# Pacing the attention stage's transfers by bytes instead of by planned time, with new instruction orders

## The chip, the cores and the metric

The kernel runs on one core of one Trainium2 chip. The metric is device time in microseconds (us) of one execution. A core has five instruction streams that matter here: PE (TensorE, matrix products), DVE (VectorE), ACT (ScalarE), POOL (GpSimd) and SP (SyncE, which here only issues transfers). All bulk transfers leave from SP's queue and are carried out by 16 DMA engines.

## What is computed

Decay attention for 8 batches, 8 heads, 576 positions and a head size of 64, and on its output a two-part mixer: one product pair along the positions, one along the channels.

```python
scores = scale * np.matmul(q, k.transpose(0, 1, 3, 2))
cum = np.cumsum(np.log(np.clip(f, 0.0001, 1.0)), axis=-1)
decay = cum[:, :, :, None] - cum[:, :, None, :]
scores = np.where(causal, -1000000000.0, scores + decay)
attn = np.exp(scores - np.max(scores, axis=-1, keepdims=True))
attn = attn / (np.sum(attn, axis=-1, keepdims=True) + 1e-09)
x = np.matmul(attn, v)                      # then (B, S, H * D)
...
h = np.maximum(x.transpose(0, 2, 1) @ w_tok1, 0.0) @ w_tok2
u = x + h.transpose(0, 2, 1)
return u + np.maximum(u @ w_ch1, 0.0) @ w_ch2
```

The channel weights come as 64-bit floats, and everything is kept to float32 precision.

## The kernel before

There are two stages. The **attention stage** takes the 64 heads as 32 pairs. For each pair SP loads q and k (`raw`, 576 KB), v (`vr`, two loads of 160 KB) and, for 26 of the pairs, a broadcast decay bias (`cb`, 576 KB). PE makes scores (L745), DVE adds the bias and takes the row minimum of the negated scores (L786), ACT takes the exponential and its row sums (L790), PE transposes (L860), ACT and DVE copy the transposed blocks out of PSUM (L870, L868) and PE multiplies by v (L889). After each second pair the inverse sums go out to memory (`recd<-rs`, L838, 5 KB each) and come back broadcast (`rb<-recd`, L843, 320 KB each), and POOL multiplies with them (L920). After each fourth pair the first mixer runs on PE (L1260, L1243), and its result goes to memory (`ud<-xt`, L1329). Beside all this the 24 weight blocks of the channel mixer are decoded from 64-bit floats: SP loads `d_raw` (L557), ACT, DVE and POOL convert (L570 to L590, L629), and the result is written back as `wd<-sg` (L638). The **channel stage** from about 405 us on streams these blocks back (`wq<-wd`, L960) into seven-product matrix multiplications (L1045 to L1047 and L1126 to L1128).

Each engine's instruction order is fixed in advance: `ORDER` (L27 on) lists, for PE, DVE, ACT, POOL and SP, the numbers of the steps in the order in which they are issued. `Plan.run` (L312) walks these lists with modelled durations. That decides which buffer slot each step gets, and so the waits between engines; the order on an engine itself comes from the table alone.

SP issues strictly in order. A transfer whose buffer is not yet free, or whose data are not yet written, holds back all transfers behind it. On top of this comes **pacing** (L318 to L328): each transfer of the attention stage may only be issued after an earlier transfer of the same queue has landed, called its hold. The loop keeps a sum `ahead` of the planned durations (`lat`, bytes divided by an assumed rate) of the transfers between the hold and the transfer, and picks as hold the latest transfer that still leaves at least `AHEAD` = 4500 ns of planned work between. The assumed rate is 300 bytes per ns for most transfers (L483), 247 for `vr` and 235 for `rb`. L1498 and L1499 turn the hold into a semaphore wait. Transfers of the channel stage have no hold.

Of the kernel before, what the change touches and what calls it, by code (L numbers as in the profile page):

```python
# [24 lines left out]
AHEAD, AHEAD_TO = 4500.0, 8  # L25
# [42 lines left out]
    ),  # L68
    DVE=(
# [187 lines left out]


class Op:
    __slots__ = ("eng", "dur", "head", "tail", "lat", "fn", "bufs", "need", "outs", "ready", "start", "idx", "port", "mode", "hold", "at_sp", "got")  # L260


class Plan:
# [48 lines left out]
    def run(self, slots):  # L312
# [6 lines left out]
        for k, o in enumerate(sent):  # L319
            if k > 1:  # L320
                ahead += sent[k - 1].lat
# [117 lines left out]
def build(nc, env, dims):  # L439
# [9 lines left out]
    p = Plan()  # L449
# [1084 lines left out]
```

## Time and profile before

| | |
|---|---|
| time, median of 3 runs | 933.07 us (929.41 to 933.65) |
| the profiled execution | 933.73 us |
| its span, first to last instruction | 931.9 us |
| PE busy, share of the span | 911.5 us, 98% |
| DVE, ACT, POOL busy | 709.0, 523.0, 234.8 us |
| moved by DMA | 242.49 MB, mean 260 GB/s |
| granted TensorE clock, mean | 0.999 of full speed |

The profiled execution lies 0.66 us above the median, and 1.8 us of it lie around the span. Busy times of different engines overlap, so they don't add up to the span; a busy PE can still contain short stalls inside a run of instructions. Waits of SP ("SPq") are waits of the issuing queue, not of the DMA engines.

### The profile page before, as it was taken

To read this page: it belongs to the slowest core of one execution; us is meant where nothing else is said; L and a number is where in the kernel's file an instruction comes from. 1 tells how busy PE (TensorE), PEld (TensorE's weight loads), DVE (VectorE), ACT (ScalarE), POOL (GpSimd) and SP (SyncE) were. 2 spreads that over 40 slices of the span, in tenths; PEclk is the share of its full clock that TensorE was granted. 3 is DMA by queue.
4 is the path that set the end of the run, shared out by engine and by line. 5 is a ranking of instruction groups with operands and counts; after the bars stand their busy time and mean duration, and the time that the engine had idled before them with its cause. 6 is when DMAs were issued, how large, how long until landed. Compare 5 with 4: busy or idle time off the path is not lost.

```text
span 931.9 us, 26826 instructions
## 1 busy us (share of the span) xinstructions
PE 911.5 (98%) x10270; PEld 794.3 (85%) x10270; DVE 709.0 (76%) x1894; ACT 523.0 (56%) x1340; POOL 234.8 (25%) x320
## 2 busy tenths in 40 slices
PE   7999899999999999999999999999999999999998
PEld 5678788888788888988888888888889999999997
DVE  7988878888788778664898369953898359954786
ACT  6979888999888989721463135512353125421242
POOL 4577567676675662100000000000000000000000
PEclk9999999999999999999999999999999999999999
DMA  8989989899998988469799888898879878887774
GB/s 247 250 277 287 308 210 321 290 297 264 301 301 251 288 265 252 134 205 329 237 308 286 269 234 236 261 302 258 261 248 287 275 227 250 248 270 232 241 249 153
DMA packets 145023, 242.49 MB, mean 260 GB/s; under 512 B 19136, under 2 KB 76736, under 8 KB 144896
## 3 DMA queue, kind: packets, MB, share of 16 engines
q1 hardware_dynamic: 144800, 240.64, 84.0%
q8 instruction: 81, 1.33, 0.6%
q14 instruction: 46, 0.38, 0.1%
q10 hardware_dynamic: 96, 0.15, 0.0%
HBM read 199.52 MB, written 41.21 MB: 258 GB/s over the span
## 4 chain that ended last, share of the span: by engine, by line
PE 89%; DVE 6%; DMA 2%; ACT 2%; issue 2%; SPq 0%; DVEq 0%; ACTq 0%
PE bank L1243 11%; PE bank L1045 9%; PE bank L1126 9%; PE bank L1127 9%; PE bank L1128 9%; PE bank L1046 9%; PE bank L1047 9%; PE bank L745 7%; PE bank L889 7%; PE bank L860 5%; DVE pr L786 3%; PE bank L1260 1%; ACT pr L790 1%; DVE pf L868 1%; DMA d_raw<-in_w_tok 1%
## 5 line engine op out<-in xcount | busy, mean ns | idle before, releaser
L487 ACT ACTIVATE st<-H 128x464 fp32r<-128x464 f32 (+1 forms) x210 | 120.7, 587 | 117.4 <-PE bank L1127 78.1
L790 ACT ACTIVATE pr<-pr,nmin 128x192 f32<-128x192 f32 (+4 forms) x320 | 176.5, 558 | 15.2 <-DVE nmin L786 14.9
L1126 PE MATMUL bank<-st,wq 128*128 128x464 f32 (+1 forms) x420 | 156.0, 371 | 0.0
L1127 PE MATMUL bank<-st,wq 128*128 128x464 f32 (+1 forms) x420 | 155.9, 371 | 0.0
L1128 PE MATMUL bank<-st,wq 128*128 128x464 f32 (+1 forms) x420 | 155.7, 371 | 0.0
L786 DVE CUSTOM_DVE_ANT_0 pr<-bank,cb 128x448 f32<-128x448 f32 (+3 forms) x260 | 108.6, 458 | 11.3 <-PE bank L751 6.7
L745 PE MATMUL bank<-raw 64*64 64x448 f32 (+6 forms) x1408 | 111.4, 397 | 5.4 <-issue 1.8
L496 DVE TENSOR_TENSOR st<-H,st 128x464 fp32r<-128x464 f32 (+1 forms) x150 | 92.3, 631 | 13.4 <-ACT st L487 13.3
L981 DVE TENSOR_TENSOR tmp<-bank,tmp 128x464 f32<-128x464 f32 (+1 forms) x80 | 50.3, 633 | 61.6 <-PE bank L1047 46.6
L889 PE MATMUL bank<-pf,vr 64*64 64x128 f32 (+3 forms) x2048 | 96.5, 315 | 0.0
L870 ACT ACTIVATE pf<-bank 128x512 f32<-128x512 f32 x152 | 84.0, 595 | 11.8 <-PE bank L860 6.3
L1128 PEld LDWEIGHTS bank<-st,wq 128*128 128x128 f32 x420 | 78.8, 188 | 9.2
L1126 PEld LDWEIGHTS bank<-st,wq 128*128 128x128 f32 x420 | 78.9, 188 | 9.0
L1127 PEld LDWEIGHTS bank<-st,wq 128*128 128x128 f32 x420 | 78.8, 188 | 8.8
L889 PEld LDWEIGHTS bank<-pf,vr 64*64 64x64 f32 x2048 | 75.2, 133 | 7.7 <-ACT pf L870 1.5
L745 PEld LDWEIGHTS bank<-raw 64*64 64x64 f32 x1408 | 54.5, 133 | 31.7 <-issue 9.8
L1071 ACT ACTIVATE H<-bank 128x464 f32<-128x464 f32 (+1 forms) x30 | 16.5, 555 | 115.2 <-PE bank L1047 109.3
L860 PE MATMUL bank<-ident,pr 64*128 64x64 f32 x1536 | 63.6, 224 | 4.3 <-issue 1.4
L860 PEld LDWEIGHTS bank<-ident,pr 64*128 64x128 f32 x1536 | 58.9, 139 | 8.1 <-DVE nmin L786 2.2
L920 POOL TENSOR_TENSOR xt<-xt,rb 128x64 f32<-128x64 f32 (+1 forms) x64 | 52.4, 837 | 48.0 <-DMA rb<-recd 26.0
L790 ACT ACTIVATION_READ_ACCUMULATOR pr<-pr,nmin 128x1 f32 (+1 forms) x320 | 62.5, 195 | 0.0
L1243 PE MATMUL bank<-t2h,ring 64*128 64x288 f32 x512 | 60.7, 304 | 1.8 <-issue 1.5
(166 smaller groups left out, 2072.8 us busy)
## 6 DMA issues: line engine op xcount, KB each, us to landing
wq<-wd SPq DMA_DIRECT2D x420, 256.0 KB
raw<-in_qk SPq DMA_DIRECT2D x32, 576.0 KB
cb<-decd SPq DMA_DIRECT2D x26, 576.0 KB
d_raw<-in_w_ch SPq DMA_DIRECT2D x48, 256.0 KB
wd<-sg SPq DMA_DIRECT2D x24, 512.0 KB
vr<-in_v SPq DMA_DIRECT2D x64, 160.0 KB
rb<-recd SPq DMA_DIRECT2D x32, 320.0 KB
wd<-sg SPq DMA_DIRECT2D x24, 384.0 KB
```

The lines of the kernel that those rows point to most:

```text
L487: nc.scalar.activation(out, in_, func, scale=scale)
L496: nc.vector.tensor_tensor(out, in_, asf(hi), op=ALU.subtract)
L745: nc.tensor.matmul(at(buf)[HALF[h], of : of + n], q[:, i0 : i0 + D], k[:, j0 : j0 + n], start=t not in (0, 1), stop=not nd, skip_group_che ...
L786: nc.vector.tensor_tensor_reduce(o, x, y, -1.0 / D**0.5, c0[:m, NS + z : NS + z + 1] if t == 5 else 3e38, op0=ALU.add, op1=ALU.min, accum_ ...
L790: nc.scalar.activation(x, x, AF.Exp, bias=E["nmin"][sm][:m, t : t + 1], scale=-1.0, accum_out=E["rec"][rm][:m, c : c + 1])
L860: nc.tensor.transpose(at(ps[s])[:, k * D : (k + 1) * D], at(pr)[r, x, :, :].rearrange("p a b -> p (a b)"), E["ident"][r, r])
L870: p.op("ACT", d_act(512), lambda src_=src_, o=o: nc.scalar.activation(o(), src_(), AF.Copy), rd=[ps[s]], wr=[(pt, s)], bufs=[ps[s], pt])
L889: nc.tensor.matmul(at(av[z])[o, 256 - w : 256], at(vr)[r, vblk(j), :], at(pt)[r, c : c + w], start=j == 4, stop=gi == 2, skip_group_check= ...
L1126: nc.tensor.matmul(o, wt[:, 0, :], h_, start=(first and x == 0), stop=False, skip_group_check=True)
L1127: nc.tensor.matmul(o, wt[:, 1, :], h_, start=False, stop=False, skip_group_check=True)
L1128: nc.tensor.matmul(o, wt[:, 0, :], l_, start=False, stop=(x == FX - 1), skip_group_check=True)
L1243: last[s] = nc.tensor.matmul(at(ps[s ^ z])[:, : width[0]], a, m, start=(z == 0 and i == 0), stop=(z == 1 and i == len(todo[s]) - 1), skip_ ...
```

## The change

The pacing no longer adds up planned durations but bytes: each transfer carries its `size`, and the hold is the latest transfer that leaves at least 1,200,000 bytes between. The first transfer of the queue, which the old sum skipped, is now counted. The flag that marks paced steps has a new name and the same condition. All five lists in `ORDER` are replaced.

```diff
-AHEAD, AHEAD_TO = 4500.0, 8
+AHEAD, PACED = 1200000, 8
...
-        "14:12 145 135:2 146 26:2 155 139 28:3 185 156 140 31:11 202 188 42 193 43:6 165 168 171 49 275 267 284 218 174 "
+        "14:12 145 135:2 146 26:2 155 139 28:3 156 185 140 31:12 193 202 43:6 188 49 165 168 171 275 267 284 174:2 211 "
...
-        o.mode, o.hold, o.at_sp = mode, None, self.batch < AHEAD_TO
+        o.mode, o.size, o.hold, o.paced = mode, 0, None, self.batch < PACED
...
-        j, ahead, sent = -1, 0.0, queue["SP"]
+        j, ahead, sent = -1, 0, queue["SP"]
         for k, o in enumerate(sent):
-            if k > 1:
-                ahead += sent[k - 1].lat
-            while j + 1 < k - 1 and ahead - sent[j + 1].lat >= AHEAD:
+            ahead += sent[k - 1].size if k else 0
+            while j + 1 < k - 1 and ahead - sent[j + 1].size >= AHEAD:
                 j += 1
-                ahead -= sent[j].lat
-            if j >= 0 and o.at_sp:
+                ahead -= sent[j].size
+            if j >= 0 and o.paced:
                 o.hold = sent[j]
...
     def dma(fn, nbytes, **k):
-        return p.op("SP", k.pop("dur", 475), fn, lat=nbytes / k.pop("rate", 300), **k)
+        o = p.op("SP", k.pop("dur", 475), fn, lat=nbytes / k.pop("rate", 300), **k)
+        o.size = nbytes
+        return o
```

305 of SP's 910 transfers are paced, in both kernels. Counted with the loop over both orders, the bytes between a hold and its transfer go from a mean of 1.57 MB (1.21 to 1.98) to a mean of 1.44 MB (1.20 to 1.78). Of the step lists, PE has 255 of 940 steps at another place (by 8 places at most), DVE 746 of 1498 (39), ACT 604 of 1020 (28), POOL 246 of 312 (13), SP 292 of 910 (47). From PE's step 2889 on, in the channel stage, PE's list is the same; the other lists agree from about there too. The numbers in buffer names below are slots; lines of the changed kernel below L484 stand two further down (L838 is now L840).

SP, the write of the inverse sums of the tenth and eleventh pair (`recd<-rs0`, at 128.66 us in the trace before), before:

```order
L720 DMA vr0_183<-in_v 64x2x320 x2
L638 DMA wd1_2_130<-sg1_156 128x3x256
L730 DMA cb0_185<-decd_118 128x1152
L838 DMA recd_119<-rs0_96 20x64 x2
L638 DMA wd1_3_131<-sg3_158 128x3x256
L557 DMA d_raw2_152<-in_w_ch1 128x512
L1329 DMA ud1_121<-xt1_145 128x1152
L843 DMA rb0_188<-recd_119 64x1280
L557 DMA d_raw2_152<-in_w_ch1 128x2x256
L843 DMA rb0_188<-recd_119 64x1280
```

SP, the same place, now:

```order
L559 DMA d_raw2_152<-in_w_ch1 128x2x256
L722 DMA vr0_183<-in_v 64x2x320
L840 DMA recd_119<-rs0_96 20x64
L1331 DMA ud1_121<-xt1_145 128x1152
L840 DMA recd_119<-rs0_96 20x64
L732 DMA cb0_185<-decd_118 128x1152
L640 DMA wd1_2_130<-sg1_156 128x4x256
L845 DMA rb0_188<-recd_119 64x1280
L732 DMA cb1_186<-decd_118 128x1152
L845 DMA rb0_188<-recd_119 64x1280
```

The bias load `cb0` has moved from ahead of the two small writes to behind them, the write `ud1` now stands between them, and two loads or writes of weight blocks have moved ahead of them. The bytes ahead of the first small write are 33.8 MB in both.

SP, the reading back of the inverse sums four pairs later (`rb`, at 187.86 us in the trace before), before:

```order
L838 DMA recd_119<-rs2_98 20x64 x2
L638 DMA wd1_5_133<-sg1_156 128x3x256
L557 DMA d_raw0_150<-in_w_ch2 128x2x256
L730 DMA cb0_185<-decd_118 128x1152
L638 DMA wd1_5_133<-sg0_155 128x4x256
L717 DMA raw2_182<-in_qk 128x1152
L557 DMA d_raw2_152<-in_w_ch2 128x2x256
L843 DMA rb0_188<-recd_119 64x1280 x2
```

SP, the same place, now:

```order
L840 DMA recd_119<-rs2_98 20x64
L1331 DMA ud2_122<-xt0_144 128x1152
L840 DMA recd_119<-rs2_98 20x64
L722 DMA vr0_183<-in_v 64x2x320
L640 DMA wd1_4_132<-sg0_155 128x3x256
L640 DMA wd1_5_133<-sg2_157 128x3x256
L559 DMA d_raw0_150<-in_w_ch2 128x2x256
L722 DMA vr0_183<-in_v 64x2x320
L732 DMA cb1_186<-decd_118 128x1152
L845 DMA rb0_188<-recd_119 64x1280
```

The second `d_raw` load no longer stands between the small writes and `rb`, and the next `raw` has moved ahead of the small writes; one `d_raw` load still stands ahead of `rb`.

## Rows read from the trace of the kernel before

**Rows 1.** Busy time and DMA share by stretch; columns: stretch, engines, clock, DMA, GB/s
```profile
0.00:50.00 50.00, 42.28 (x738) 29.40 (x740) 44.30 (x182) 37.60 (x110) 26.36 (x48) 1.00 0.87 257
50.00:100.00 50.00, 48.97 (x1017) 41.79 (x1012) 43.98 (x164) 44.38 (x133) 37.76 (x50) 1.00 0.90 275
100.00:150.00 50.00, 45.37 (x934) 39.39 (x935) 40.98 (x149) 41.16 (x123) 33.32 (x44) 1.00 0.93 274
150.00:200.00 50.00, 49.76 (x1029) 41.41 (x1027) 43.21 (x160) 44.51 (x130) 32.79 (x45) 1.00 0.94 299
200.00:250.00 50.00, 48.93 (x1016) 41.95 (x1016) 41.68 (x148) 45.76 (x137) 33.86 (x44) 1.00 0.94 288
250.00:300.00 50.00, 48.50 (x1030) 40.28 (x1024) 41.94 (x159) 41.91 (x127) 30.57 (x42) 1.00 0.88 270
300.00:350.00 50.00, 49.51 (x1022) 42.51 (x1022) 39.13 (x150) 43.94 (x134) 30.28 (x39) 1.00 0.91 275
350.00:405.00 55.00, 54.92 (x1012) 48.94 (x1014) 37.96 (x119) 39.56 (x113) 9.86 (x12) 1.00 0.68 200
405.00:450.00 45.00, 45.00 (x222) 40.19 (x219) 27.41 (x50) 11.34 (x22) 0.00 (x0) 1.00 0.82 260
450.00:930.00 480.00, 478.25 (x2286) 428.42 (x2284) 348.43 (x622) 172.86 (x318) 0.00 (x0) 1.00 0.83 256
```

**Rows 2.** PE's timeline, its idle times over 1 us between 95 and 135 us
```profile
101.72 0.46 PE L1260 MATMUL bank<-ident,xt 64*128 64x64 f32 x8 [1.78 <-issue]
115.66 0.48 PE L745 MATMUL bank<-raw 64*64 64x320 f32 x4 [1.36 <-issue]
122.66 0.40 PE L1243 MATMUL bank<-t2h,ring 64*128 64x288 f32 x1 [1.48 <-issue]
```

**Rows 3.** Waits of SP's queue, 0 to 405 us: in total, times, longest
```profile
SPq L557 <- DVE d_g L590: 24.7, 12, 4.4
SPq L838 <- DVE rs L831: 24.5, 10, 5.6
...
SPq L638 <- DMA d_raw<-in_w_ch: 8.2, 5, 2.6
SPq L717 <- DMA d_raw<-in_w_ch: 7.8, 5, 2.5
...
SPq L638 <- DMA rb<-recd: 6.6, 5, 2.5
```

**Rows 4.** SP's timeline at four places: start, duration, what
```profile
107.02 0.67 SPq L838 DMA_DIRECT2D recd<-rs  x2
...
112.03 1.13 SPq L843 DMA_DIRECT2D rb<-recd  x2
...
122.55 0.43 SPq L730 DMA_DIRECT2D cb<-decd  x1
128.66 0.68 SPq L838 DMA_DIRECT2D recd<-rs  x2
...
187.27 0.55 SPq L557 DMA_DIRECT2D d_raw<-in_w_ch  x1
...
223.14 0.67 SPq L838 DMA_DIRECT2D recd<-rs  x2
...
226.13 1.26 SPq L843 DMA_DIRECT2D rb<-recd  x2
```

**Rows 5.** The columns of rows 1, by the us, where SP waited
```profile
127.00:128.00 1.00, 1.00 (x19) 0.48 (x19) 1.00 (x4) 0.82 (x3) 1.00 (x2) 1.00 0.15 60
128.00:129.00 1.00, 1.00 (x16) 0.66 (x12) 1.00 (x3) 1.00 (x5) 0.04 (x1) 1.00 0.00 0
129.00:130.00 1.00, 1.00 (x20) 0.81 (x20) 0.52 (x2) 1.00 (x5) 0.00 (x0) 1.00 0.05 10
```

**Rows 6.** DVE's timeline, the first reading of that `cb`
```profile
141.11 0.22 DVE L786 CUSTOM_DVE_ANT_0 pr<-bank,cb 64x64 f32<-64x64 f32 x1
```

**Rows 7.** POOL's timeline, the wait for `rb`
```profile
194.88 3.09 POOL L920 TENSOR_TENSOR xt<-xt,rb 128x512 f32<-128x512 f32 x4 [2.92 <-DMA rb<-recd]
```

**Rows 8.** Waits of PE, 0 to 405 us, the only one for a transfer
```profile
PE bank L745 <- DMA raw<-in_qk: 1.4, 1, 1.4
```

More of the change, by code (lines that the diff above doesn't have):

```diff
@@ L259 @@
 class Op:
-    __slots__ = ("eng", "dur", "head", "tail", "lat", "fn", "bufs", "need", "outs", "ready", "start", "idx", "port", "mode", "hold", "at_sp", "got")
+    __slots__ = ("eng", "dur", "head", "tail", "lat", "fn", "bufs", "need", "outs", "ready", "start", "idx", "port", "mode", "size", "hold", "paced", "got")
 class Plan:
```

397 rows, old and new, of tables (ACT, DVE, PE, POOL) are left out of this document.

## The prediction

> **What bounds the kernel now.** I read the busy times by stretch first [rows 1]. Up to 405 us runs the attention stage, after it the channel stage. In the channel stage PE is busy 45.00 of 45 and 478.25 of 480 us, and its order there is the same but for the first steps, so I look for nothing there. In the attention stage PE's idle time is what the eight rows leave over: 7.72, 1.03, 4.63, 0.24, 1.07, 1.50, 0.49 and 0.08 us, together 16.8 us. The first 7.7 us hold the start, where there is nothing to multiply yet. Of the 4.63 us between 100 and 150 us, 1.78 + 1.36 + 1.48 = 4.62 us are three gaps marked "issue" [rows 2]: PE waited for nothing that the profile shows, no semaphore and no transfer. So without the start and these three, about 4.4 us of plain idle time are left in 405 us. The engines beside PE are full too: between 50 and 350 us DVE is busy 78 to 88% and ACT 82 to 92%, and the DMA engines 88 to 94%, at 270 to 299 GB/s. The stage is four tight engines coupled by small buffers, and PE is the one that ends it.
>
> Then the waits of SP's queue [rows 3], because the change acts there. Two kinds of wait for a compute engine lead: 24.7 us in 12 waits for a weight block's decode, 24.5 us in 10 waits for the inverse sums. Those come from the order. Waits for a transfer, among which are all the holds, come in many small rows; the largest are 8.2, 7.8 and 6.6 us, of five waits each, the longest of a row being 2.5 or 2.6 us. Last, who waits for what SP brings: PE waits for a transfer once in the stage, 1.4 us [rows 8].
>
> **Term 1, pacing by bytes.** Between hold and transfer there are now 1.44 MB on the mean where there were 1.57 MB, and 1.20 MB at least. At 280 GB/s, the middle of the rates in rows 1, the mean difference is 0.13 MB / 280 GB/s = 0.46 us: that much later a transfer is issued where the hold is its last wait. It costs only where the DMA engines run dry meanwhile. What must be covered is the time from a landing to the next transfer's work. The nearest rows: the small write `recd` and the read `rb` that needs it. At 223.14 us the two writes are issued, done at 223.81, and `rb` follows at 226.13: 2.3 us, with other issues between, so an upper bound in a queue with little in it. At 107.02 it is 112.03 - 107.69 = 4.3 us, with a full queue in front, which contains the data of others [rows 4]. With 1.2 MB behind the hold, the engines have 1.2 MB / 280 GB/s = 4.3 us of work, 2.0 us more than the 2.3. So the cover is the transfers already queued, and it is still there at the smallest window. If the cover were gone, the price is 0.46 us for each long wait: the three largest rows hold 15 waits, so 15 x 0.46 = 6.9 us, if each reached PE. That is the upper end. Below zero: a later issue brings no data sooner, but fewer bytes queued could shorten the three issue gaps, if data in the queues is what delays PE there. In proportion (0.13 of 1.57 MB, 8% of 4.62 us) that gains 0.4 us. I take +0.4 us, one exposed delay, near the row of PE's single wait: one in the stage.
>
> Here a rule of the Trainium skill speaks against the change. In "DMA: Bandwidth & Descriptors", section "Anatomy of one DMA — SWDGE (gpsimd) path", a transfer's time is a fixed part of about 2.0 us, mostly completion, and bytes at 436 GB/s. At that rate 1.2 MB would last only 2.75 us, hardly more than the round trip, and the smallest windows would leave the engines dry; by it the sum would take the upper end of term 1 and not its middle. The rate in this trace is 299 GB/s at best over 50 us [rows 1], so the trace does not agree with the rule's rate for this mix of transfers, and its 2.0 us are below the 2.3 us read here.
>
> **Term 2, the orders.** The same instructions run on each engine, so busy time stays, and only waits can change. At the first place SP blocked before `recd` for the inverse sums: `cb` was issued at 122.55, `recd` only at 128.66, a wait of 5.6 us [rows 3, 4], and the DMA engines fell to 0.15, 0.00 and 0.05 of their share from 127 to 130 us, while PE stayed busy for all three us [rows 5]. Now `cb` is behind `recd`, `ud` is between the two small writes, and as many bytes stand ahead of them, so the engines run dry just as before unless the sums come sooner. Behind the waiting `recd` now stand `ud`, the second `recd`, `cb`, `wd` and `rb`. The `cb` that moved back was first read at 141.11 us [rows 6], 18.6 us after its issue; issued at about 130 it still has 11 us, against the 4.3 us that a round trip took in a full queue. I price this move at nothing, hidden by DVE's and PE's earlier work; if that cover is gone, it costs DVE up to the wait's 5.6 us.
>
> At the second place `d_raw` waited for its buffer until 187.27 us, and `rb` stood behind it; POOL waited 2.92 us for `rb` before 194.88 [rows 4, 7]. Now one `d_raw` load less stands between, but another is still ahead. At best POOL gets these 2.92 us back. PE's idle time in that stretch is 0.24 us in all [rows 1], so PE gains 0.24 us at most unless stalls hide inside its busy time. So this too is worth nothing I could measure.
>
> The other moves are too many to price one by one. Their bounds: they cannot gain more plain idle time than there is, 4.4 us, and the largest single loss that rows show is SP's 5.6 us wait coming up once more, with PE behind it. I take 0, since no row names a wait on PE of more than 1.4 us that the order could take away, and because the waits that go at one place come back at another: SP's blocking writes are all still there.
>
> **The sum.** The profiled execution took 933.73 us. Term 1 adds 0.4 and term 2 adds 0: 934.1 us. The profiled execution lies 0.66 us over the median of the runs shown, so for the median I forecast 933.5 us. Its own range goes down by term 2's 4.4 and term 1's 0.8 (from +0.4 to -0.4) to 928.3, and up to 937.7, the point from which a loss would be told from no change and the rivals below begin.
>
> **Rivals.** (A) A new blocked head of SP's queue, slower. In the new order a transfer that PE needs soon gets behind a `recd` or `d_raw` that waits. Price: one 5.6 us wait with the queue dry, all of it reaching PE, 933.1 + 5.6 = 938.7 us. For: 22 such waits stand in the two leading rows, and `ud`, which waits for the mixer's sums, now stands ahead of the second `recd`. Against: PE stayed busy while the engines were dry before, and PE waited for a `raw` once in the stage, 1.4 us [rows 5, 8]. It decides from the point where a `raw` or `cb` lands after its first use would have begun. Chance 0.11.
>
> (B) The window runs dry, slower. The holds of 1.20 MB release too late, and the engines run dry before the next transfer starts. All 15 long waits of term 1 get 0.46 us longer: 933.1 + 6.9 = 940 us. For: SP's waits for transfers grow with load, and the engines are at 88 to 94% already. Against: 2.0 us of cover. It decides where DMA share between 100 and 300 us falls below 0.88 with SP waiting for a transfer. Chance 0.06.
>
> (C) The new orders take out stalls inside PE's busy time, faster. Between 50 and 350 us PE is called busy nearly throughout, but its weight loads are busy 39 to 43 of 50 us [rows 1], so short stalls may hide there. If the orders regain 2% of those 300 us, that is 6 us: 933.1 - 6 = 927 us. For: so many steps moved, on all engines. Against: no one row shows a wait this large on PE. Chance 0.13.
>
> (D) The pacing doesn't do what it says: the holds are so seldom the last wait that the window's size changes nothing, and only the orders act. That gives 933.1 us and falls inside the forecast, so it shares its chance of 0.70.
>
> **How the numbers follow.** What the runs of this kernel can tell from no change is about 0.5%, 4.7 us: 928.4 to 937.7 us. The forecast with D has 0.70, A and B, both over 937.7, have 0.17 together, C has 0.13. So faster 0.13, same 0.70, slower 0.17. For 8 in 10 the range must reach a part of the cases on both sides: 928.5 to 939.5 us leaves out most of C and of B.
>
> **What would show it.** Term 1 is right if SP's waits for transfers keep their sum and DMA share between 100 and 300 us stays at 0.88 to 0.94; wrong if the share falls while those waits grow. Term 2 is right if PE's idle time up to 350 us stays within a few us of 16.7, if SP's wait at `recd` near 128 us is still there, and if POOL's wait near 195 us shrinks without PE noticing. The end of the attention stage near 405 us is the mark: if it moves by more than 4.7 us, the forecast is wrong, and the stretch in which PE's work first runs ahead or behind tells which rival it was.

## The result and the profile after

The changed kernel takes 937.99 us (median of 8 runs, 935.1 to 942.57), the kernel before, run beside it, 933.36 us (median of 8 runs, one of which took 1951.73 us and is left out of the ratio). The ratio is 1.0051, 95% interval 1.0028 to 1.0074: slower by half a per cent. The forecast was 933.5 us with a range of 928.5 to 939.5, so the time lies in the range, but just past the 937.7 us up to which I had called it no change. The profiled execution took 937.82 us, its span is 936.0 us (931.9 before).

Busy time by stretch in the changed kernel: stretch, PE, weight loads, DVE, ACT, POOL (each with its count), granted clock, DMA share, GB/s. Its last three rows are single microseconds.

```profile
0.00:50.00 50.00, 40.85 (x739) 29.06 (x741) 44.31 (x176) 37.27 (x109) 26.61 (x47) 1.00 0.83 254
50.00:100.00 50.00, 48.25 (x955) 41.91 (x955) 43.61 (x159) 42.89 (x130) 35.42 (x47) 0.97 0.86 274
100.00:150.00 50.00, 48.63 (x1009) 41.19 (x1003) 44.16 (x162) 43.68 (x130) 36.42 (x49) 1.00 0.95 279
150.00:200.00 50.00, 48.79 (x998) 39.85 (x1000) 41.62 (x152) 43.76 (x131) 30.47 (x42) 1.00 0.99 296
200.00:250.00 50.00, 49.35 (x1032) 42.76 (x1026) 44.59 (x153) 45.37 (x137) 38.31 (x49) 1.00 0.92 278
250.00:300.00 50.00, 46.64 (x1008) 39.41 (x1003) 40.01 (x150) 39.80 (x120) 28.96 (x40) 1.00 0.98 293
300.00:350.00 50.00, 48.94 (x996) 42.31 (x992) 39.92 (x153) 45.19 (x138) 29.85 (x39) 1.00 0.95 269
350.00:405.00 55.00, 53.94 (x1021) 47.59 (x1022) 37.65 (x124) 39.49 (x115) 10.43 (x12) 1.00 0.63 189
...
127.00:128.00 1.00, 1.00 (x13) 0.29 (x7) 1.00 (x3) 1.00 (x5) 1.00 (x2) 1.00 0.29 95
128.00:129.00 1.00, 1.00 (x24) 0.86 (x26) 1.00 (x4) 1.00 (x4) 1.00 (x1) 1.00 0.47 182
129.00:130.00 1.00, 1.00 (x41) 0.98 (x37) 1.00 (x5) 1.00 (x4) 0.06 (x1) 1.00 1.05 398
```

Against [rows 1], stretch by stretch, PE idles more by 1.43, 0.72, -3.26, 0.97, -0.42, 1.86, 0.57 and 0.98 us: 19.6 us in 405 us where there were 16.8. The clock row adds a part: between 50 and 100 us the granted clock is 0.97 of full speed, because from 53.07 to 56.48 us PE ran at 1.2 and not 2.4 GHz. Those 3.4 us at half rate cost up to 1.7 us. Together that is up to 2.9 + 1.7 = 4.6 us, against 4.1 us more span. The last matrix product of the attention stage ends at 409.3 us and not at 405.6; what is left to the end is 526.7 and 526.3 us. So 3.7 of the 4.1 us are lost in the attention stage.

The waits of SP's queue in the changed kernel, 0 to 405 us: in total, times, longest.

```profile
SPq L559 <- DVE d_g L592: 24.3, 15, 4.0
SPq L840 <- DVE rs L833: 14.8, 7, 4.2
...
SPq L640 <- DMA vr<-in_v: 10.0, 6, 3.0
SPq L640 <- DMA raw<-in_qk: 7.5, 6, 2.7
```

Where [rows 3] had 24.5 us in 10 waits for the inverse sums there are now 14.8 in 7. All waits for transfers together grew from 91.7 us in 90 waits to 118.9 us in 109. On the whole the DMA engines did not run dry for it: their share between 100 and 350 us is 0.92 to 0.99.

SP's timeline of the changed kernel at the two places of the prediction: start, duration, what.

```profile
127.43 0.31 SPq L840 DMA_DIRECT2D recd<-rs  x1
...
128.18 0.36 SPq L840 DMA_DIRECT2D recd<-rs  x1
128.58 0.76 SPq L732 DMA_DIRECT2D cb<-decd  x1
...
184.88 0.47 SPq L845 DMA_DIRECT2D rb<-recd  x1
185.94 0.57 SPq L559 DMA_DIRECT2D d_raw<-in_w_ch  x1
...
188.97 0.60 SPq L845 DMA_DIRECT2D rb<-recd  x1
```

And POOL's wait at the second place:

```profile
196.93 0.60 POOL L922 TENSOR_TENSOR xt<-xt,rb 128x64 f32<-128x64 f32 x2 [4.76 <-DMA d_raw<-in_w_ch]
```

The first place behaves as foreseen: SP still blocks before `recd`, for 2.9 us where it was 5.6 (the profile puts 2.4 us of it down to a `raw` load, but DVE's reciprocal ended only at 126.86 + 0.54 = 127.40 us, just before `recd` went), and the engines still run low (0.29 and 0.47 against 0.15 and 0.00 in [rows 5]) while PE stays busy. At the second place the first `rb` does go 3 us earlier than in [rows 4], but the second is now behind a `d_raw` and two `vr` and goes at 188.97, where it went at 188.60. POOL's wait grew from the 2.92 us of [rows 7] to 4.76.

The largest waits of PE in the changed kernel, 0 to 405 us:

```profile
PE bank L862 <- DVE nmin L788: 3.5, 7, 0.8
PE bank L891 <- issue: 1.9, 2, 1.7
...
PE bank L862 <- issue: 1.7, 1, 1.7
PE bank L1262 <- POOL xt L922: 1.6, 2, 1.1
PE bank L747 <- DMA raw<-in_qk: 1.4, 1, 1.4
PE bank L891 <- DMA vr<-in_v: 1.3, 1, 1.3
...
PE bank L747 <- DVE xt L910: 1.1, 1, 1.1
```

Beside the one wait of [rows 8], which is the same, PE now waits for POOL's product with the inverse sums (L1262 needs `xt`), for a `vr` and longer for DVE. There are still gaps marked "issue", for which the profile shows no cause; the two longest now lie before 293.31 and 350.77 us. No single row shows 4 us.

### The profile page after: what moved, and what is told of

The parts are those of the page before. It is cut to its first block, busy times and chain, and to the rows that moved or that the text cites. A ratio compares the mean times of both kernels' runs of the same rounds, so it can differ in the third digit from the quotient of the medians.

```text
span 936.0 us, 26831 instructions
## 1 busy us (share of the span) xinstructions
PE 912.3 (97%) x10270; PEld 796.0 (85%) x10270; DVE 712.2 (76%) x1894; ACT 522.2 (56%) x1340; POOL 236.5 (25%) x320
## 4 chain that ended last, share of the span: by engine, by line
PE 76%; DMA 8%; DVE 7%; ACT 3%; issue 2%; POOL 2%; SPq 1%; DVEq 0%; POOLq 0%; ACTq 0%
PE bank L1047 9%; PE bank L1128 9%; PE bank L1129 9%; PE bank L1130 9%; PE bank L1048 9%; PE bank L1049 9%; PE bank L1245 8%; PE bank L747 4%; PE bank L891 4%; PE bank L862 3%; DVE pr L788 3%; DMA rb<-recd 2%; ACT pr L792 2%; DMA d_raw<-in_w_ch 1%; DMA vr<-in_v 1%
## 5 line engine op out<-in xcount | busy, mean ns | idle before, releaser
L792 ACT ACTIVATE pr<-pr,nmin 128x448 f32<-128x448 f32 (+4 forms) x320 | 176.8, 560 | 12.6 <-DVE nmin L788 12.0
L747 PE MATMUL bank<-raw 64*64 64x448 f32 (+6 forms) x1408 | 109.1, 397 | 3.4 <-DMA raw<-in_qk 1.4
L495 POOL TENSOR_TENSOR sg<-d_g,sg 128x512 fp32r<-128x512 f32 x48 | 61.8, 1295 | 1.3
```

What stands on the lines that cost most here:

```text
L747: nc.tensor.matmul(at(buf)[HALF[h], of : of + n], q[:, i0 : i0 + D], k[:, j0 : j0 + n], start=t not in (0, 1), stop=not nd, skip_group_che ...
L792: nc.scalar.activation(x, x, AF.Exp, bias=E["nmin"][sm][:m, t : t + 1], scale=-1.0, accum_out=E["rec"][rm][:m, c : c + 1])
```

## The experiments

Letters in the expectations: W, the smaller window costs the time; O, the new orders cost it; C, the clock costs it; N, the clock is a bystander. Where an experiment changes the holds, they are recomputed after the planning, so that orders and buffer slots stay exactly those of the kernel named. The two kernels of mixed order are planned with the changed kernel's own pacing, so their buffer slots are those of neither kernel; order and slots are not told apart there. Columns and waits are read as above, from one profiled execution of each kernel; SP's waits are those from 0 to 405 us.

### The changed kernel again

No edit. 

> The changed kernel itself once more, beside the other three. 936 to 940 us, with a stretch at half clock near 51 to 57 us in its profile and a mean granted clock of 0.998 or less in nearly every run.

Measured: 938.1 us against 933.2, ratio 1.0045 (1.0024 to 1.0067), 12 runs. The loss is there again. This profile shows three stretches at 1.2 GHz, at 22.6 to 26.0, 53.3 to 56.7 and 319.5 to 326.4 us, where the first profile of the same kernel had only the one near 53 us, and its execution took 942.6 us; two runs with a mean granted clock of 1.000 took 934.24 us each. So part of the loss changes its place from execution to execution.

### Old orders with the new window, and new orders with the old window

```diff
     order = p.run(slots_of())
+    sent = [o for o in order if o.eng == "SP"]
+    j, ahead = -1, 0
+    for k, o in enumerate(sent):
+        ahead += sent[k - 1].size if k else 0
+        while j + 1 < k - 1 and ahead - sent[j + 1].size >= 1200000:
+            j += 1
+            ahead -= sent[j].size
+        o.hold = sent[j] if j >= 0 and o.at_sp else None
```

The lists of the kernel before stand; only the holds are chosen anew, by bytes.

> The orders and buffer slots of the kernel before, with only the holds chosen anew by 1.2 MB. If the shorter window costs the time (W), this is slower than before by about the 4.6 us of the whole change, 937 to 939 us, and SP's waits for transfers up to 405 us grow from 91.7 us towards 119 us. If the orders cost it (O), it is within 2 us of before, 931 to 935 us, even if SP's waits grow.

Measured: 932.43 us against 933.82, ratio 0.9996 (0.9977 to 1.0014). SP's waits for transfers rise to 126.2 us in 112, more than in the changed kernel, and cost nothing.

The second kernel is the reverse: all lists new, and after the planning the loop of the kernel before, with `lat` and 4500 ns.

> The orders and buffer slots of the changed kernel, with the holds chosen as before, by 4500 ns of planned time. W: the loss goes, 931 to 935 us. O: it stays, 936 to 940 us, and the chain of waits still runs through rb, cb, vr and raw transfers for some 8% of the span.

Measured: 935.77 us, ratio 1.0018 (0.9994 to 1.0043). Not told from no change by itself, so it was run once more beside the last two experiments:

> The new orders with the old holds (4500 ns of planned work) a second time, to tell an interaction from an effect of the orders alone. Orders alone (O): 1.004 to 1.005, about 937.5 us. Interaction (the new orders lose only with the smaller window): 1.000 to 1.002, about 934 to 935 us, with SP's waits for transfers near 102 us as in the first such run and not near 119 us.

Measured: 937.47 us against 934.34, ratio 1.0041 (1.0010 to 1.0073), with 99.4 us of waits for transfers. So the window alone costs nothing that the runs can tell, and the orders alone cost about 0.3%, the middle of the two. Whether the smaller window adds the remaining 0.2% on top of the new orders is within the intervals and stays open; PE's idle times, in the table further down, speak for it.

### No holds at all

```diff
     order = p.run(slots_of())
+    sent = [o for o in order if o.eng == "SP"]
+    for o in sent:
+        o.hold = None
```

New orders: 

> The orders and slots of the changed kernel with no holds at all. W: as fast as before or faster, 929 to 934 us, since no issue is held back. O: 936 to 940 us, since the blocked heads of SP's queue stay where the order puts them.

Old orders: 

> The kernel before with no holds at all. W: faster than before by 1 to 4 us, as its own window of 4500 ns costs something too. O: the same as before within 2 us. If pacing helps by keeping the queues short, it is slower, 935 us or more.

Measured: 944.03 us, ratio 1.0119 (1.0083 to 1.0154), and 940.35 us, ratio 1.0088 (1.0057 to 1.0119), with SP's waits for transfers down to 18.1 and 22.4 us. Of what I had expected only the last case for the old orders comes out: without any pacing the new orders are 8.3 us slower than with the old holds (935.77) and the old orders 6.5 us slower than the kernel before (933.82). The waits are worth having. Why issuing without holds is dearer is not isolated by these runs.

### Extra matrix products to keep the clock up

```diff
+                if n2 in (2, 3, 4):
+                    for _ in range(5):
+                        nc.tensor.matmul(at(ps[0])[:64, :48], E["ident"][:, :64], E["ident"][:, :48], start=True, stop=True, skip_group_check=True)
```

The same five stand ahead of the first product with v; 60 products in all, whose result is overwritten. In the changed kernel: 

> The changed kernel with five small matmuls put ahead of each group of transposes and ahead of the first product with v of the third to fifth pair (60 in all, about 0.075 us each by the start's dummies, 4.5 us of PE time), into banks that the same step overwrites; they need no data, so they run where PE waits. If the half-clock stretch near 53 us comes from PE's idle time before it and costs time (C), the clock stays whole and the time falls to 933 to 936 us. If the clock is a bystander (N), the time stays at 937 to 939 us or grows by up to 4.5 us, even when the clock stays whole.

In the kernel before: 

> The same 60 matmuls in the kernel before. C: the runs of before with a clock of 0.996 to 0.998 (about 935.5 us) vanish, the median falls to 931 to 933 us. N: 933 to 938 us.

Measured: 941.42 us, ratio 1.0103 (1.0062 to 1.0143), and 937.55 us, ratio 1.0060 (1.0039 to 1.0081), both against 933.2. Neither profile has a stretch at 1.2 GHz any more. The products cost about 4 us of their own. The difference between the two kernels, 3.9 us, is about as large as without them, so the loss doesn't go away with the clock. How much of it the clock carries this pair can't say: the two intervals overlap, and four of the six runs of the changed kernel with extra products still have a mean granted clock below 1.000.

The clocks of the other runs say more. Of the 79 runs of the kernel before that were made beside these experiments, 33 have a mean granted clock of 1.000, and they take 932.6 us on the mean. Of the 20 runs of the changed kernel, 2 do, with the 934.24 us each. Over all runs the mean clock is 0.9987 before and 0.9963 now. At 1.2 GHz the granted share is 0.5, so the difference of 0.0024 is 0.0024 x 2 x 936 = 4.5 us more at half rate, which cost up to 2.2 us; this is an estimate. So about half of the loss is paid at the lower clock, and about half without it.

### A smaller and a larger window, old orders

The loop is that of the old orders with the new window, with another limit (2400000 in the second kernel):

```diff
+        while j + 1 < k - 1 and ahead - sent[j + 1].size >= 900000:
```

> The orders and slots of before with a window of 0.9 MB. At 280 GB/s this lasts 3.2 us, against the 2.3 us read for a round trip in a queue with little in it. If the window runs dry below about 4 us (W), this is slower than before by 4 us or more; if 2.3 us is all that must be covered, it is within 2 us of it.

Measured: 943.04 us against 933.2, ratio 1.0099 (1.0065 to 1.0134); SP waits 174.8 us in 135 for transfers. In its windows PE falls behind between 100 and 300 us, at full clock; with the same orders and 1.2 MB it was busy 49.75 and 48.34 us in these two:

```profile
150.00:200.00 50.00, 45.40 (x926) 38.06 (x924) 39.22 (x146) 40.86 (x121) 28.98 (x39) 1.00 0.90 268
...
250.00:300.00 50.00, 46.48 (x954) 39.31 (x952) 39.43 (x142) 39.65 (x119) 27.90 (x36) 1.00 0.92 273
```

> The old orders with holds that leave 2.4 MB in between, twice the new window; 2.4 MB last 8.6 us at 280 GB/s. 1.2 MB took 932.4 us, no holds 940.4, 0.9 MB 943.0. If the loss without holds comes from many bytes in the queue that delay the transfer PE needs next, 2.4 MB lies between: about 935 to 938 us, ratio 1.002 to 1.005, SP's waits for transfers well under 90 us. If only a few far-ahead issues do the harm that any hold prevents, 2.4 MB costs nothing: 933 us, ratio 0.999 to 1.001.

Measured: 937.14 us against 934.34, ratio 1.0049 (1.0025 to 1.0072). So with the old orders 0.9 MB costs 1.0%, 1.2 MB nothing, 2.4 MB 0.5% and no limit 0.9%. There is a best window between. Counted as means, as for the two rules, 0.9, 1.2 and 2.4 MB are 1.12, 1.43 and 2.62 MB, so the old rule (1.57 MB) and the new one (1.44 MB) both lie in the range that costs nothing with these orders.

### Which half of the new orders

All five lists of `ORDER` were cut at the steps planned before 190 us. The first kernel has these steps in the new order and all later ones in the old; the rest is the changed kernel.

> The changed kernel, except that every step planned later than 190 us stands in the old order again; byte holds of 1.2 MB throughout. In the two traces the changed kernel lost about 2 us before 65 us and about 2.5 us between 288 and 389 us. Theory E (the loss comes from the early steps): about 936 to 938 us, ratio 1.003 to 1.005, and the sibling with the halves exchanged about 934. Theory L (from the late steps): about 934 us, ratio 1.000, the sibling 937. If both halves carry their share: about 935.5 us and ratio 1.002 for each of the two.

The sibling takes the old order first, then the new:

> The changed kernel, except that every step planned before 190 us stands in the old order; byte holds of 1.2 MB throughout. Theory E (early steps lose): about 934 us, ratio 1.000. Theory L (late steps lose): 936 to 938 us, ratio 1.003 to 1.005. Both: about 935.5 us, ratio 1.002. If the two siblings' losses add up to clearly less than 0.5%, the loss needs the whole order, and no place in it can be named.

Measured: 934.48 us, ratio 0.9997 (0.9971 to 1.0022), for new then old; 938.33 us, ratio 1.0055 (1.0032 to 1.0077), for old then new; both against 934.34 us, 12 runs each. The intervals don't touch. **With the new window, the loss lies in the order of the steps after 190 us**, all of it within the error; the early half of the new orders, with the places at 128 and 187 us that I had looked at, costs nothing on balance.

The profiles show more. I take PE's first transposition of the mixer near 199 us, the end of the attention stage, and PE's idle time from 200 to 404 us (204 us less its busy time in that window):

| kernel | first | end | between | PE idle |
|---|---|---|---|---|
| before | 199.9 | 405.6 | 205.7 us | 3.1 us |
| old orders, new window | 198.3 | 404.0 | 205.7 | 3.8 |
| new then old | 201.8 | 406.9 | 205.1 | 3.2 |
| new, old window, twice | 200.4; 200.8 | 406.5; 409.1 | 206.1; 208.3 | 3.1; 4.0 |
| changed kernel, twice | 201.3; 202.6 | 409.3; 414.2 | 208.0; 211.6 | 6.1; 6.8 |
| old then new | 198.2 | 409.9 | 211.7 | 6.0 |

Every kernel with the new late half is above every one with the old. PE's idle time draws another line: it is higher only where the new late half meets the new window, by 2 to 4 us. With the old window the new late half waits no more than the old one, and the 208.3 us of one such profile hold 3.4 us at 1.2 GHz (336.2 to 339.6 us). So in these profiles the two parts of the change act together; each kernel has one or two profiles, so this is not settled by them.

Windows of old then new:

```profile
300.00:350.00 50.00, 45.78 (x862) 38.60 (x864) 35.34 (x119) 38.85 (x114) 31.60 (x39) 0.93 0.94 258
...
315.00:320.00 5.00, 2.32 (x28) 1.69 (x30) 1.53 (x4) 1.22 (x4) 4.92 (x7) 0.59 0.93 277
320.00:325.00 5.00, 5.00 (x92) 4.20 (x85) 2.91 (x7) 2.42 (x9) 0.88 (x1) 0.72 0.66 192
...
316.00:317.00 1.00, 0.00 (x0) 0.00 (x0) 0.00 (x0) 0.00 (x0) 1.00 (x3) 0.50 1.12 272
...
322.00:323.00 1.00, 1.00 (x22) 0.87 (x18) 0.58 (x1) 0.00 (x0) 0.00 (x0) 0.62 0.91 263
```

and of new then old:

```profile
300.00:350.00 50.00, 49.45 (x1025) 42.65 (x1026) 39.10 (x151) 44.03 (x134) 29.88 (x39) 1.00 0.91 276
```

862 products against 1025 between 300 and 350 us: the hole is at 313 to 323 us. From 316 to 317 us POOL alone is busy; PE, DVE and ACT have all stopped. What PE waits for, in old then new (PE's timeline):

```profile
314.81 0.27 PE L1263 MATMUL bank<-ident,xt 64*128 64x64 f32 x2 [1.23 <-POOL xt L923]
317.77 1.01 PE L1263 MATMUL bank<-ident,xt 64*128 64x64 f32 x14 [2.68 <-POOL xt L923]
```

In new then old the same step starts as one run, after an idle time of 0.42 us that a copy by ACT ended:

```profile
317.12 0.71 PE L1264 MATMUL bank<-ident,xt 64*128 64x64 f32 x16 [0.42 <-ACT pf L874]
```

POOL's multiplication in old then new:

```profile
313.09 1.67 POOL L923 TENSOR_TENSOR xt<-xt,rb 128x64 f32<-128x64 f32 x2 [4.20 <-PE bank L863]
...
316.46 1.26 POOL L923 TENSOR_TENSOR xt<-xt,rb 128x512 f32<-128x512 f32 x1
```

In new then old it begins at 307.17 us:

```profile
307.17 1.56 POOL L924 TENSOR_TENSOR xt<-xt,rb 128x64 f32<-128x64 f32 x2 [1.30 <-issue]
```

POOL's 4.20 us are put down to PE, which had long been done. The same step in the repeated changed kernel, in its chain of work that ended last, names the releaser: the `rb` transfer of 9.99 us.

```profile
305.12 9.99 DMA rb<-recd
...
318.78 1.23 POOL xt L922
320.01 0.04 issue
320.05 1.01 PE bank L1262 x13
```

And why `rb` is late stands in SP's timeline, in old then new:

```profile
293.29 0.57 SPq L560 DMA_DIRECT2D d_raw<-in_w_ch  x1
293.91 1.55 SPq L641 DMA_DIRECT2D wd<-sg  x2
296.51 1.50 SPq L841 DMA_DIRECT2D recd<-rs  x2
...
300.06 0.60 SPq L720 DMA_DIRECT2D raw<-in_qk  x1
...
302.48 1.51 SPq L846 DMA_DIRECT2D rb<-recd  x2
```

and in new then old:

```profile
292.87 0.30 SPq L842 DMA_DIRECT2D recd<-rs  x1
...
294.29 0.30 SPq L842 DMA_DIRECT2D recd<-rs  x1
...
298.58 1.31 SPq L847 DMA_DIRECT2D rb<-recd  x1
...
300.57 0.52 SPq L847 DMA_DIRECT2D rb<-recd  x1
```

In the new late order a `d_raw` load and two writes of weight blocks stand ahead of the writes of the inverse sums. DVE had these sums at 293.04 us (a reciprocal of 0.55 us from 292.49), and they went out 3.5 us later; 1.0 us of it SP waited, by the profile, for the landing of a `ud`. Between `recd` and `rb` there are now `vr`, `wd`, `d_raw`, `raw` and `vr`, 160 + 384 + 256 + 576 + 160 = 1,536 KB, where the old order has two `vr` and one `wd`, 704 to 832 KB. So `rb` is issued later and lands behind more data, POOL begins 5.9 us later, although PE was 3.5 us ahead at the transposition near 199 us, and the reserve before PE's transposition is gone. Reading this chain from the traces is as far as it goes: moving only these few transfers back was not tried, so that they are the whole of the loss is not shown.

Three other profiles say that they are not the whole of it. The new orders with the old window have the same transfers in the same order here, and `rb` goes at 302.2 us in both profiles; yet PE doesn't wait for `xt`. In the second of the two (SP, then PE):

```profile
302.22 1.18 SPq L845 DMA_DIRECT2D rb<-recd  x2
...
314.89 0.88 PE L1262 MATMUL bank<-ident,xt 64*128 64x64 f32 x16
```

So the late order takes the reserve away, and whether PE then waits differs between executions or hangs on the window. The first profile of the changed kernel loses nothing at 315 us either (POOL ends at 316.39, PE starts at 317.59, 1.2 us of reserve). It has the same thing 50 us earlier: the second `recd` went at 249.20 us, where it was 241.35 before, and PE waits 1.13 us for `xt` until 265.94. That is about a third of its 3 us more idle time; the longest pause that the kernel before doesn't have there, 1.71 us until 350.77, is marked "issue", and its cause stays open.

The half clock comes right behind these waits. In old then new PE was idle or nearly so from 314 to 318 us, the granted clock was 0.50, that is 1.2 GHz, from 316 us on, and came back to 2.4 GHz within the slice at 322 us. PE worked again from 317.77 us, so some 5.0 us of work ran at half rate and lost up to 2.5 us. With the two waits, 1.23 + 2.68 = 3.9 us, that makes 6.4 us, about the 6.0 us between the 211.7 us of the table and the 205.7 of the kernel before. The Trainium skill, in "TensorE: Matmul & The Clock Gate", section "HAM oscillation — how this bites in real kernels", tells of a kernel whose TensorE waits for a transfer between bursts of work and starts the next burst at the lower clock. The trace agrees, with the 0.50 after the two waits; here the wait was for POOL, and through it for `rb`.

## Why the prediction was right where it was, and wrong where it wasn't

**Term 1, pacing by bytes (+0.4 us, bounds -0.4 to +6.9): right, taken alone.** With the old orders it measured 0.9996, that is -0.4 us with an interval of -2.1 to +1.3. Its mark came out half: the DMA share stayed up, but SP's waits for transfers did not keep their sum, they grew by 27 us, and by 34 us in the kernel with the old orders, at no cost. The cover is there, but it is thinner than I worked out. At 0.9 MB, or 900,000 / 280 GB/s = 3.2 us, there should still have been 0.9 us over the 2.3 us that I took for a round trip; it cost 9.8 us. So by this reckoning more than 3.2 us have to be covered; the 4.3 us of [rows 4] would fit, but no run measures it. The upper end was too low as well: it counts the 15 waits of the three largest rows, while the stage has 90 waits for transfers.

**The rule of the Trainium skill that spoke against it** ("DMA: Bandwidth & Descriptors", "Anatomy of one DMA — SWDGE (gpsimd) path": 436 GB/s, by which 1.2 MB last 2.75 us) would have put term 1 at its upper end, 6.9 us. That isn't what 1.2 MB did. The warning itself was good for a slightly smaller window: 0.9 MB took more than those 6.9 us.

**Term 2, the orders (0, bounds -4.4 to +5.6): this is the step that missed.** It measured +0.18% and +0.41% by itself, +0.45% to +0.55% with the new window (+4.2 to +5.1 us). The value lies inside the bound and near its upper end. The reason I gave for 0 was "the waits that go at one place come back at another". That counts SP's blocked time, and SP's blocked time did fall, from 24.5 to 14.8 us at the inverse sums. What the late half of the orders took away was reserve: the time from DVE's sums to POOL's multiplication is 20.0 us in old then new and 14.8 us in new then old, and it grew where the two places I had looked at don't lie. I looked at 128 and 187 us, the loss begins after 190 us. Two things more were missing from the sum. It adds the terms as if each acted for itself, and PE's idle times speak against that. And it holds nothing for the granted clock, which carries about half of the loss.

**That the time fell into the range** is owed to the room that the range leaves for rivals. 937.99 us is 4.5 us over the forecast, of which neither term foresaw any part.

**The first place** was right: the wait at `recd` near 128 us is still there, shorter, and PE doesn't notice it. **The second place** was wrong in its sign: POOL's wait grew by 1.8 us instead of shrinking. I had counted one `d_raw` less ahead of `rb`, but only the first of the two `rb` loads gained by it. PE noticed a little of it: of its 1.6 us of waits for `xt`, 0.5 us lie here.

**Rival A, a new blocked head of SP's queue (938.7 us, chance 0.11)** is nearest to what happened, in size (937.99) and in kind: a transfer needed soon got behind others. It was not a `raw` or `cb` that came late, as I had it, but `rb`; and the queue wasn't dry but full. My reason against it, that PE waited for a transfer once in the stage [rows 8], looked only at direct waits of PE; this one reaches PE through POOL. That reason was too weak to bear a chance as low as 0.11. **B** did not decide at 1.2 MB (the share stayed at 0.86 or more between 50 and 350 us). **C**, hidden stalls taken out, did not come; the 3.3 us gained between 100 and 150 us are no merit of the new orders, since the profile of the old orders with the new window also shows 48.69 us there, so the old order alone doesn't make the three gaps of [rows 2]. **D** is refuted in one part: the holds are often the last wait, and taking them away costs 6.5 us and more.

**The sum's other marks.** PE's idle time up to 350 us is 18.6 us against 16.7, within the few us allowed; the stage's end moved by 3.7 us, under the 4.7 that I had set as the limit. Both were set so wide that a loss of half a per cent passes them.

## What to carry to other kernels

Follow a chain of small transfers from its producer to its last consumer, through every queue, and compare the time left over at the end in both orders; the wait of the issuing queue says little. When an order is rewritten over the whole program, exchange halves of it on the chip: two runs placed a loss of half a per cent that no single row of the profile showed. A limit on the bytes ahead had an optimum here, and no limit was as dear (0.9%) as one of 0.9 MB (1.0%). Before a clock stretch is called a bystander, compare the granted clocks of all runs of both kernels, not only of the profiled ones.

## What the runs showed of the hardware that was not expected

- Issuing transfers without a limit was slower than the kernel before, by 0.9% (old orders) and 1.2% (new ones), and 2.4 MB in between cost 0.5%. That more data in front of urgent transfers is the cause was not isolated and stays open.
- Between 0.9 and 1.2 MB of data ahead there is a step of 1.0% of the time, though the DMA share falls by only a few hundredths (0.86 to 0.92 between 50 and 350 us, against 0.89 to 0.97 with the same orders and 1.2 MB).
- Stretches at 1.2 GHz appear after short idle times of PE in some executions and not in others, 3.4 us long at 53 us and up to 6.9 us long at 319 us; both kernels with 60 extra products had none in their profiles, but paid about 4 us for the products. Of the runs of the kernel before, 33 of 79 have a mean granted clock of 1.000, of the changed kernel 2 of 20.
